# A first batch with distances and scores first, and a last output tile in two halves

## The chip, the cores and the metric

The kernel runs on one NeuronCore of a Trainium2 chip. The metric is the device time of one execution in microseconds (us), the median over several executions.

## The reference, cut to what matters

```python
# q, k, v: [8 batches, 8 heads, 576 positions, 64]; window 128
scores = q @ k.T / 8 + slopes[h] * -(i - j)        # ALiBi: a slope for each head
scores = where(0 <= i - j < 128, scores, -1e9)     # causal, sliding window
attn   = softmax(scores)
x      = (attn @ v) as [8 * 576, 8 * 64]           # 4608 tokens x 512
h      = x @ w_in                                  # 512 -> 2048
out    = (h * cos(h)) @ w_out                      # 2048 -> 512, float32
```

## The kernel before

Attention and the two matrix products of the feed-forward part are one stream of work. A batch's attention is nine *units*: four pairs of heads times two halves of the sequence (G = 0 and 1, 256 positions each), and one unit `"t"` for the last 64 positions of all heads. A unit is scores (TensorE, line 486, or 477 for the tail), exponential (ScalarE, line 516 or 508), multiplication by a table that holds ALiBi and the window (VectorE, line 532 or 525), P·V (TensorE, lines 564 and 567), division by the row sum (VectorE, lines 602 and 604), and a turn into the transposed tokens `xT` (TensorE, line 632, and a copy; later by DMA). The feed-forward part goes by nine chunks of 512 tokens: `moe1` (line 668; `moe1_half`, line 691, for chunk 0, in halves of 256 tokens) gives h, ScalarE takes its cosine, VectorE multiplies, and `moe2` (line 714) makes four output tiles of 128 tokens x 512 columns, each copied from PSUM (lines 720, 722) and stored (line 726).

For batches 0 and 1, q and k come as rows (`load_qk`, line 321) and are transposed on TensorE against an identity matrix `ident` (`qk_transposes`, line 434; copies in lines 448 and 449). Batch 0 comes in two pieces for each of q and k: positions 0 to 255 and 256 to 575. The first piece is all that the four units of G = 0 need; the others need both.

The table `EM` of ALiBi and window comes from a matrix of distances `dif` (GpSimd, lines 375 to 382), by eight exponentials on ScalarE (line 404) and copies on VectorE (lines 409 and 414). All loads are issued by GpSimd, in the order in which the program records them. They convert float32 to bfloat16 on the way.

The order on the other engines isn't the program's: `Plan.schedule` is a list scheduler that runs when the program is built. Each operation has a cost (`occ`, the time it holds its engine, and `lat`, the time to its result), a priority `pri` (lower first) and dependencies by names of buffers; the scheduler keeps a model of when each engine is free and when transfers land (`WIRE0`, `lat` of the loads), and repeatedly takes what can start first. Where an operation may run on ScalarE or VectorE, it also picks the engine. `emit` then writes the engines' programs in that order, with semaphores. So a changed cost changes no work, but may change an order. PSUM's eight banks are named `SB` (scores, four), `UB` (P·V, two) and `OB` (output tiles, two).

Of the kernel before, what the change touches and what calls it, by code (L numbers as in the profile page):

```python
# [7 lines left out]
ACTF = mybir.ActivationFunctionType  # L8
# [3 lines left out]
B, H, S, D = 8, 8, 576, 64  # L12
# [22 lines left out]
class Plan:  # L35
# [2 lines left out]

    SWITCH = 95
    TABLE = 1330  # L40
    WIRE0 = 3700

    def __init__(self, nc, ctx):
        self.nc, self.ctx = nc, ctx
# [41 lines left out]


    def schedule(self):
        free = {e: 0 for e in ENG}
        wire = {e: self.WIRE0 for e in ENG}  # L90
        mode, table = 0, None
        tables = sorted({o.table for o in self.all if o.table is not None})
        left = {t: sum(o.table == t for o in self.all) for t in tables}
        avail = []

        def reach(o, e):
            t = 0
            for d, data in o.preds.items():
                if data == ORDER or self.held(d, data, e):
                    t = max(t, d.start + d.occ)  # L100
                elif d.dma is None and d.eng[0] == e:
                    t = max(t, d.end + 28)
                else:
                    t = max(t, d.end + (53 if e == "pe" else 36))
            return t
        for o in self.all:
            if o.npred == 0:
                avail.append(o)
        order = []
        while avail:  # L110
            phase = next((t for t in tables if left[t]), None)
            best = None
            for e in ENG:
                cand = []
                for o in avail:
# [12 lines left out]
                key = (st, o.pri, o.seq)  # L128
                if best is None or key < best[0]:
                    best = (key, e, o)  # L130
            (st, _, _), e, o = best
            avail.remove(o)
            if o.table is not None and o.table != table:
                st += self.TABLE
            if len(o.eng) > 1:
                o.fn, o.occ, o.lat = o.fn[e], o.occ[e], o.lat[e]
                o.eng = (e,)
            o.start = st
            free[e] = st + o.occ
# [101 lines left out]
def bass_alibi_sliding__then__act_gcu_kernel(  # L241
# [8 lines left out]
    with ExitStack() as ctx:  # L250
# [62 lines left out]
        def piece_keys(which, b, n):  # L313
            return [("qB", which, 0), ("qB", which, 1)] if b else [("qB", which, n)]

        def load_qk(which, src, b, n=0):
            t0, R, _ = PIECES[b][n]
            c0 = 64 * (t0 // 32)
            rows = bass.AP(src.tensor, src[b].offset + 64 * t0,
                           [[64 * R, 32], [64 * S, H], [1, 64 * R]])  # L320
            op("pool", [lambda e: e.dma_start(qB[which][:, :, c0:c0 + 64 * R], rows)],  # L321
               w=piece_keys(which, b, n), dma=f"ld{which}{n}", occ=800, lat=161 * R)

        def load_v(b, order=range(NBLK)):
            for t in order:
                rows = 128 if t < 4 else 64
                op("pool", [lambda e, t=t, rows=rows: e.dma_start(  # L327
                    vp[b % 2][0:rows, t, :, 0:64],
                    v[b, :, 128 * t:128 * t + rows, :].rearrange("h p d -> p h d"))],
                   r=[("vinit", b % 2)], w=[("v", b % 2, t)], dma=f"ldv{b % 2}{t}",  # L330
                   occ=900, lat=7 * rows)

        def load_nat(which, src, b):
            fns = []
# [31 lines left out]
               w=[("wo", u)], dma=f"wo{u}", occ=800, lat=2650)  # L366


        def constants():
            sel = ["sel"]  # L370
            op("pool", lambda e: e.memset(ident[:, :], 1.0), w=["ident"] + sel)
            op("pool", lambda e: e.affine_select(
                ident[:, :], ident[:, :], pattern=[[1, 128]], compare_op=ALU.is_equal,
                fill=0.0, base=0, channel_multiplier=-1), r=["ident"], w=["ident"] + sel, occ=350)
            op("pool", lambda e: e.iota(dif[:, :, :], pattern=[[128, 2], [-1, 128]], base=-128,
                                        channel_multiplier=1,
                                        allow_small_or_imprecise_dtypes=True),
               w=["dif"] + sel, occ=350)
            op("pool", lambda e: e.affine_select(
                dif[:, 0, :], dif[:, 0, :], pattern=[[-1, 128]], compare_op=ALU.is_ge,  # L380
                fill=-1.0e6, base=-1, channel_multiplier=1), r=["dif"], w=["dif"] + sel, occ=350)
            op("pool", lambda e: e.affine_select(
                dif[:, 1, :], dif[:, 1, :], pattern=[[1, 128]], compare_op=ALU.is_ge,
                fill=-1.0e6, base=0, channel_multiplier=-1), r=["dif"], w=["dif"] + sel, occ=350)
# [35 lines left out]
        def qk_transposes(b, which, n, part, banks):  # L420
# [8 lines left out]
            def f(e):  # L429
# [6 lines left out]
                                qB[which][:, y, c0 + 64 * j:c0 + 64 * j + 64], ident[:, :])  # L436
                return ins
            num = jj[1][1] - jj[0][0]
            op("pe", f, r=piece_keys(which, b, n) + ["ident"], w=[("B", x) for x in banks],
               occ=56 * num if b else 110 * num, lat=56 * num + 170 if b else 110 * num + 250,  # L440
               mode=2, pri=3)
            for i, (j0, j1) in enumerate(jj):
                o = tr[which][b % 2][:, :].rearrange("p (k t) -> p k t", k=NPAIR)[
# [237 lines left out]
        def moe1_half(c, hf, f2, bank):  # L681
# [6 lines left out]
            for i in range(2):  # L688
# [15 lines left out]
               r=[("cos", ci)], w=[("B", bank)] + [("g", gi, 2 * f2 + i, hf) for i in range(2)],  # L704
               occ=606, lat=692, pri=3)

        def moe2(c):
            gi = c % 2
            for t in range(4):
                tg = 4 * c + t  # L710
                bank = OB[tg % 2]
                oi = tg % NOB
                for fc in range(NFC):
                    op("pe", lambda e, t=t, fc=fc, bank=bank: e.matmul(  # L714
                        ps[:, bank, :], gT[gi][:, fc, 128 * t:128 * t + 128], w_out[:, fc, :],
                        start=(fc == 0), stop=(fc == NFC - 1)),
                       r=[("g", gi, fc, t // 2), ("wo", fc // 4)], w=[("B", bank)], occ=216, lat=379,
                       pri=6)
# [13 lines left out]
        def attention(us, phase):  # L732

            for g in range(0, len(us), 2):
# [6 lines left out]
                else:  # L741
# [2 lines left out]
                        exps(u, n, 2 * phase + 2)  # L744
                    for u in two:
                        mask(u)
                sets = [list(zip(two, UB))]
                if any(u[1] == "t" for u in two):
                    sets = [[s] for s in sets[0]]
                for set_ in sets:  # L750
# [13 lines left out]


        load_qk("q", q, 0, 0)
        load_qk("k", k, 0, 0)
        constants()
        load_qk("q", q, 0, 1)
        load_qk("k", k, 0, 1)  # L770
        load_v(0)
        masks()
        for n in range(2):
            qk_transposes(0, "q", n, 0, OB)
            qk_transposes(0, "k", n, 0, OB if n else UB)
        for u in range(4):
            load_w_in(u)
        load_qk("q", q, 1)
# [34 lines left out]
                    load_nat("k", k, next_t)  # L813
            moe2(c)
        R.schedule()
        R.emit(final=[f"st{i}" for i in range(NOB)])

# [1 line left out]
_INS = ['q', 'k', 'v', 'moe_w_in', 'moe_w_out']  # L819
# [24 lines left out]
```

The softmax here doesn't subtract the row's maximum and nothing guards it: scores larger than these inputs give would overflow.

## Time and profile before

| | |
|---|---|
| time, median of 3 | 321.82 us (321.12 to 321.84) |
| span of the profiled execution | 319.1 us |
| TensorE busy | 306.3 us, 96% of the span |
| ScalarE busy | 204.1 us, 64% |
| VectorE busy | 187.5 us, 59% |
| GpSimd busy | 95.8 us, 30% |
| moved by DMA | 37.82 MB, 119 GB/s over the span |

The profile shows one execution. Engines are PE (TensorE), PEld (its weight loads), DVE (VectorE), ACT (ScalarE), POOL (GpSimd) and SP. A row of 40 digits gives the busy share of an engine in tenths, a digit for each fortieth of the span (8 us here). In a line of the timeline stand the start in us, the duration in us, engine, line of the kernel, operation, and what is written from what; "[1.69 <-DMA ...]" is the time that the engine sat idle before it, and what ended that wait. "x16" is a count. [...] matmuls in a row overlap: 128x512 ones last 379 ns and follow each other every 216 ns.

### The profile page before, as it was taken

The numbers are of one execution on the slowest core, as the hardware profiler recorded it, in microseconds if no ns is written. First come the engines' busy times: TensorE is split into PE (matmuls) and PEld (weight loads), VectorE is DVE, ScalarE is ACT, GpSimd is POOL, SyncE is SP. The second block draws the span as 40 slices with busy tenths as digits, with TensorE's granted clock in tenths as the row PEclk, the third lists the DMA queues.
The fourth block names the chain that finished last, engine by engine and source line by source line (L and its number), as shares of the span: only waits on it lengthen the run. The fifth ranks groups of instructions, "written<-read, shape, count | busy, mean of one in ns | idle before, by whom it ended". The sixth has DMA issues, their size and how long they took to land.

```text
span 319.1 us, 6207 instructions
## 1 busy us (share of the span) xinstructions
PE 306.3 (96%) x2450; PEld 152.9 (48%) x2450; DVE 187.5 (59%) x413; ACT 204.1 (64%) x297; POOL 95.8 (30%) x123
## 2 busy tenths in 40 slices
PE   2799999999999999999999999999999999999995
PEld 2468745445544554455445444544444444444442
DVE  3788758776686777669775656655653650334000
ACT  5697866886688696966678567665674662443211
POOL 7997142254537581564508100000000000000000
PEclk9999999999999999999999999999999999999999
DMA  6999999999999999999999992131022001101121
GB/s 89 179 207 210 204 160 192 146 153 169 177 123 163 167 190 150 178 164 180 125 140 148 136 147 68 55 69 44 2 73 68 34 0 68 66 0 68 66 93 71
DMA packets 144476, 37.82 MB, mean 119 GB/s; under 512 B 134208, under 2 KB 139328, under 8 KB 144448
## 3 DMA queue, kind: packets, MB, share of 16 engines
q0 software_dynamic: 99616, 18.36, 78.1%
q1 hardware_dynamic: 44832, 19.08, 29.0%
q8 instruction: 19, 0.31, 0.4%
q14 instruction: 9, 0.07, 0.1%
HBM read 36.70 MB, written 9.44 MB: 145 GB/s over the span
## 4 chain that ended last, share of the span: by engine, by line
PE 90%; DMA 6%; POOL 1%; issue 1%; DVE 0%; ACT 0%; POOLq 0%; ACTq 0%
PE ps L714 40%; PE ps L668 35%; DMA qrows<-in_q_dram 6%; PE ps L486 5%; PE ps L564 3%; PE ps L691 2%; PE ps L567 2%; PE ps L434 1%; PE ps L632 1%; PE ps L477 1%; PE ps L551 1%; PE ps L553 1%; POOL w_inb L357 1%; POOL qrows L321 0%; POOL krows L321 0%
## 5 line engine op out<-in xcount | busy, mean ns | idle before, releaser
L714 PE MATMUL ps<-w_outb,gT 128*128 128x512 bf16 x576 | 138.8, 379 | 0.0
L668 PE MATMUL ps<-xT,w_inb 128*128 128x512 bf16 x512 | 116.8, 379 | 0.4 <-DVE xnat L604 0.3
L677 DVE TENSOR_TENSOR gT<-ps,cos 128x512 bf16<-128x512 f32 x128 | 81.0, 685 | 50.2 <-PE ps L714 41.1
L673 ACT ACTIVATE cos<-ps,halfpi 128x512 f32<-128x512 f32 x128 | 81.3, 687 | 37.8 <-PE ps L714 18.6
L714 PEld LDWEIGHTS ps<-w_outb,gT 128*128 128x128 bf16 x576 | 53.7, 98 | 58.7 <-issue 1.9
L668 PEld LDWEIGHTS ps<-xT,w_inb 128*128 128x128 bf16 x512 | 47.2, 98 | 61.2 <-DVE gT L677 6.0
L516 ACT ACTIVATE p<-ps 128x768 bf16<-128x768 f32 (+1 forms) x64 | 55.6, 919 | 22.3 <-PE ps L486 18.6
L532 DVE TENSOR_TENSOR p<-p,emask 128x768 bf16<-128x768 bf16 (+1 forms) x64 | 38.3, 615 | 7.3 <-ACT p L516 6.9
L327 POOL DMA_DIRECT2D vp<-in_v_dram x40 | 33.8, 872 | 23.0 <-PE ps L567 12.2
L720 ACT ACTIVATE ob<-ps 128x512 f32<-128x512 f32 x25 | 15.0, 599 | 37.1 <-PE ps L714 37.0
L337 POOL DMA_DIRECT2D qnat<-in_q_dram x30 | 25.2, 875 | 28.8 <-DMA qt<-qnat 28.8
L337 POOL DMA_DIRECT2D knat<-in_k_dram x30 | 25.3, 877 | 27.6 <-DMA kt<-knat 25.2
L604 DVE TENSOR_TENSOR xnat<-ps,rec 128x256 bf16<-128x256 f32 x64 | 24.4, 420 | 0.7 <-DVE rec L602 0.4
L486 PE MATMUL ps<-qt,kt 64*128 64x128 bf16 (+1 forms) x320 | 19.0, 243 | 0.7 <-ACT p L516 0.7
L602 DVE RECIPROCAL rec<-ps 128x4 f32<-128x4 f32 x64 | 8.2, 168 | 18.1 <-PE ps L567 17.8
L564 PEld LDWEIGHTS ps<-vp,p 128*128 128x128 bf16 x256 | 15.4, 97 | 7.0 <-issue 3.5
L564 PE MATMUL ps<-vp,p 128*128 128x65 bf16 x256 | 18.2, 193 | 0.2 <-DVE p L532 0.2
L486 PEld LDWEIGHTS ps<-qt,kt 64*128 64x128 bf16 x320 | 11.2, 95 | 12.4 <-issue 5.1
L567 PE MATMUL ps<-vp,p 128*128 128x65 bf16 x192 | 17.0, 193 | 0.0
L691 PE MATMUL ps<-xT,w_inb 128*128 128x256 bf16 x128 | 16.0, 273 | 0.3 <-ACT xT L641 0.3
L722 DVE COPY ob<-ps 128x512 f32<-128x512 f32 x11 | 7.6, 689 | 12.7 <-PE ps L714 12.7
L567 PEld LDWEIGHTS ps<-vp,p 128*128 128x128 bf16 x192 | 13.3, 97 | 0.6
(51 smaller groups left out, 166.7 us busy)
## 6 DMA issues: line engine op xcount, KB each, us to landing
out_dram<-ob SPq DMA_DIRECT2D x36, 256.0 KB, 2.1
vp<-in_v_dram POOLq DMA_DIRECT2D x32, 128.0 KB, 9.1
qnat<-in_q_dram POOLq DMA_DIRECT2D x24, 128.0 KB, 7.2
knat<-in_k_dram POOLq DMA_DIRECT2D x24, 128.0 KB, 5.0
w_inb<-in_moe_w_in_dram POOLq DMA_DIRECT2D x4, 512.0 KB, 10.3
w_outb<-in_moe_w_out_dram POOLq DMA_DIRECT2D x4, 512.0 KB, 22.1
qrows<-in_q_dram POOLq DMA_DIRECT2D x1, 576.0 KB, 15.1
krows<-in_k_dram POOLq DMA_DIRECT2D x1, 576.0 KB, 17.1
```

What stands on the lines that cost most here:

```text
L327: op("pool", [lambda e, t=t, rows=rows: e.dma_start(vp[b % 2][0:rows, t, :, 0:64], v[b, :, 128 * t:128 * t + rows, :].rearrange("h p d -> ...
L337: fns.append(lambda e, t=t, rows=rows: e.dma_start(nat[which][0:rows, t, :, :], src[b, :, 128 * t:128 * t + rows, :].rearrange("h p d -> p ...
L486: ins = e.matmul(ps[:, banks[x], c0:c1], keys_ap(b, x, pr, kc), query_ap(b, x, pr, qb, 128 * nb), start=True, stop=True)
L516: op("act", lambda e: e.activation(P[i][:, :, lo:512], src_[:, :, lo:512], ACTF.Exp, scale=0.125), w=held + [("P", i)], occ=920 if G else ...
L532: op("dve", lambda e: e.tensor_tensor(P[i][:, :, lo:512], P[i][:, :, lo:512], EM[:, h0:h1 + 1, lo:512], ALU.mult), r=[("P", i), ("EM", h0) ...
L564: ins = e.matmul(o, P[i][:, x, d0:d0 + 128], V[:, kc, h, 0:65], start=True, stop=not two)
L567: ins = e.matmul(o, P[i][:, x, p0:p0 + 128], V[:, kc - 1, h, 0:65], start=False, stop=True)
L604: op("dve", lambda e: e.tensor_tensor(o, U[:, :, :, 0:64], rv[:, :, :, None].broadcast_to([128, 2, 2, 64]), ALU.mult), r=[("rec", n % 2)], ...
L668: op("pe", lambda e, kc=kc: e.matmul(ps[:, bank, :], w_in[:, kc, 128 * fc:128 * fc + 128], xT[:, kc, r0:r0 + CH], start=(kc == 0), stop=(k ...
L673: op("act", lambda e: e.activation(cosb[ci][:, :], ps[:, bank, :], ACTF.Sin, bias=halfpi[:, 0:1]), r=["halfpi"], w=[("B", bank), ("cos", c ...
L677: op("dve", lambda e: e.tensor_tensor(gT[gi][:, fc, :], ps[:, bank, :], cosb[ci][:, :], ALU.mult), r=[("cos", ci)], w=[("B", bank), ("g", ...
L714: op("pe", lambda e, t=t, fc=fc, bank=bank: e.matmul(ps[:, bank, :], gT[gi][:, fc, 128 * t:128 * t + 128], w_out[:, fc, :], start=(fc == 0 ...
```

## The change

It has three parts. First, GpSimd makes the distances right behind the first two loads and the identity only behind the third load, and the transposes of the second pieces of batch 0 are made to wait for the copies of the first k piece, so that scores of the first units come ahead of them; the first P·V pair uses banks `OB` instead of `UB`, and the k transposes always use `UB`. The aim is to begin attention on the first pieces while the second are on their way. Second, the scheduler's model of the start is changed: the times at which engines begin (`BEGIN`), TensorE operations that take twice as long in the first 18.5 us (`COLD`), and some costs. These are numbers for the scheduler and no work on the chip. Third, the last output tile is computed in two halves of 256 columns in two banks, each with a copy and a store of its own (`moe2_last`), so that the first half is copied and stored while the second is computed.

```diff
-    WIRE0 = 3700
+    WIRE0 = 3450
+    BEGIN = {"pe": 1000, "act": 2100, "dve": 1000, "pool": 1330, "sp": 1000}
+    COLD = 18500
...
-        free = {e: 0 for e in ENG}
+        free = dict(self.BEGIN)
...
+            if e == "pe" and st < self.COLD:
+                o.lat += o.occ
+                o.occ *= 2
...
-        def constants():
-            sel = ["sel"]
-            op("pool", lambda e: e.memset(ident[:, :], 1.0), w=["ident"] + sel)
+        def identity():
+            op("pool", lambda e: e.memset(ident[:, :], 1.0), w=["ident"], occ=290)
...
+        def distances():
             op("pool", lambda e: e.iota(dif[:, :, :], pattern=[[128, 2], [-1, 128]], base=-128,
...
-            op("pe", f, r=piece_keys(which, b, n) + ["ident"], w=[("B", x) for x in banks],
-               occ=56 * num if b else 110 * num, lat=56 * num + 170 if b else 110 * num + 250,
+            op("pe", f, r=piece_keys(which, b, n) + ["ident"] + (
+                   [("tr", "k", 0, j) for j in (0, 4)] if n else []), w=[("B", x) for x in banks],
+               occ=58 * num, lat=58 * num + 170,
...
+        def moe2_last(c, t, oi):
+            gi, row = c % 2, CH * c + 128 * t
+            for hf, bank in enumerate((OB[1], UB[0])):
+                cols = slice(256 * hf, 256 * hf + 256)
+                for fc in range(NFC):
+                    op("pe", lambda e, fc=fc, bank=bank, cols=cols: e.matmul(
+                        ps[:, bank, 0:256], gT[gi][:, fc, 128 * t:128 * t + 128],
+                        w_out[:, fc, cols], start=(fc == 0), stop=(fc == NFC - 1)),
...
+                op("sp", [lambda e, cols=cols: e.dma_start(out[row:row + 128, cols],
+                                                           ob[oi][:, cols])],
+                   r=[("ob", oi, hf)], dma=f"sl{hf}", occ=60, lat=300)
...
-                sets = [list(zip(two, UB))]
+                sets = [list(zip(two, OB if phase < 0 and g == 0 else UB))]
...
         load_qk("q", q, 0, 0)
         load_qk("k", k, 0, 0)
+        distances()
+        load_qk("q", q, 0, 1)
+        identity()
+        load_qk("k", k, 0, 1)
         constants()
-        load_qk("q", q, 0, 1)
-        load_qk("k", k, 0, 1)
...
-            qk_transposes(0, "k", n, 0, OB if n else UB)
+            qk_transposes(0, "k", n, 0, UB)
```

More of the change, by code (lines that the diff above doesn't have):

```diff
@@ L88, in schedule @@
     def schedule(self):
-        free = {e: 0 for e in ENG}
+        free = dict(self.BEGIN)
         wire = {e: self.WIRE0 for e in ENG}
-        mode, table = 0, None
+        mode, table = 0, 0
         tables = sorted({o.table for o in self.all if o.table is not None})
@@ L321, in load_qk @@
             op("pool", [lambda e: e.dma_start(qB[which][:, :, c0:c0 + 64 * R], rows)],
-               w=piece_keys(which, b, n), dma=f"ld{which}{n}", occ=800, lat=161 * R)
+               w=piece_keys(which, b, n), dma=f"ld{which}{n}", occ=740, lat=159 * R)
         def load_v(b, order=range(NBLK)):
@@ L330, in load_v @@
                    r=[("vinit", b % 2)], w=[("v", b % 2, t)], dma=f"ldv{b % 2}{t}",
-                   occ=900, lat=7 * rows)
+                   occ=900, lat=740 * rows // 100)
         def load_nat(which, src, b):
@@ L366, in load_w_out @@
                w=[("wo", u)], dma=f"wo{u}", occ=800, lat=2650)
-        def constants():
-            sel = ["sel"]
-            op("pool", lambda e: e.memset(ident[:, :], 1.0), w=["ident"] + sel)
+        def identity():
+            op("pool", lambda e: e.memset(ident[:, :], 1.0), w=["ident"], occ=290)
             op("pool", lambda e: e.affine_select(
                 ident[:, :], ident[:, :], pattern=[[1, 128]], compare_op=ALU.is_equal,
-                fill=0.0, base=0, channel_multiplier=-1), r=["ident"], w=["ident"] + sel, occ=350)
+                fill=0.0, base=0, channel_multiplier=-1), r=["ident"], w=["ident"], occ=360)
+        def distances():
             op("pool", lambda e: e.iota(dif[:, :, :], pattern=[[128, 2], [-1, 128]], base=-128,
@@ L377, in constants @@
                                         allow_small_or_imprecise_dtypes=True),
-               w=["dif"] + sel, occ=350)
+               w=["dif"], occ=450)
             op("pool", lambda e: e.affine_select(
                 dif[:, 0, :], dif[:, 0, :], pattern=[[-1, 128]], compare_op=ALU.is_ge,
-                fill=-1.0e6, base=-1, channel_multiplier=1), r=["dif"], w=["dif"] + sel, occ=350)
+                fill=-1.0e6, base=-1, channel_multiplier=1), r=["dif"], w=["dif"], occ=430)
             op("pool", lambda e: e.affine_select(
                 dif[:, 1, :], dif[:, 1, :], pattern=[[1, 128]], compare_op=ALU.is_ge,
-                fill=-1.0e6, base=0, channel_multiplier=-1), r=["dif"], w=["dif"] + sel, occ=350)
+                fill=-1.0e6, base=0, channel_multiplier=-1), r=["dif"], w=["dif"], occ=400)
+        def constants():
             for i in range(2):
@@ L705, in moe1_half @@
                occ=606, lat=692, pri=3)
+        def moe2_last(c, t, oi):
[6 more added lines that the diff above has]
+                        w_out[:, fc, cols], start=(fc == 0), stop=(fc == NFC - 1)),
+                       r=[("g", gi, fc, t // 2), ("wo", fc // 4)], w=[("B", bank)], occ=108,
+                       lat=271, pri=6)
+                op(("act", "dve"),
+                   {"act": lambda e, bank=bank, cols=cols: e.activation(
+                       ob[oi][:, cols], ps[:, bank, 0:256], ACTF.Copy),
+                    "dve": lambda e, bank=bank, cols=cols: e.tensor_copy(
+                        ob[oi][:, cols], ps[:, bank, 0:256])},
+                   w=[("B", bank), ("ob", oi, hf), ("ob", oi)],
+                   occ={"act": 281, "dve": 320}, lat={"act": 384, "dve": 405}, pri=6)
+                op("sp", [lambda e, cols=cols: e.dma_start(out[row:row + 128, cols],
+                                                           ob[oi][:, cols])],
+                   r=[("ob", oi, hf)], dma=f"sl{hf}", occ=60, lat=300)
         def moe2(c):
@@ L712, in moe2 @@
                 oi = tg % NOB
+                if tg == NTOK // 128 - 1:
+                    moe2_last(c, t, oi)
+                    continue
                 for fc in range(NFC):
@@ L815, in bass_alibi_sliding__then__act_gcu_kernel @@
         R.schedule()
-        R.emit(final=[f"st{i}" for i in range(NOB)])
+        R.emit(final=[f"st{i}" for i in range(NOB)] + ["sl0", "sl1"])
 _INS = ['q', 'k', 'v', 'moe_w_in', 'moe_w_out']
```

## The prediction

> **What bounds the kernel now.** I read the page first: how full TensorE is, and what the chain of waits is made of.
>
> ```profile
> PE   2799999999999999999999999999999999999995
> PEclk9999999999999999999999999999999999999999
> PE 90%; DMA 6%; POOL 1%; issue 1%; DVE 0%; ACT 0%; POOLq 0%; ACTq 0%
> ```
>
> TensorE is full in all slices but the first two and the last. An edit can gain only in the ramp, in the tail, or by taking work off TensorE, and none is taken off here. Next, the busy time of the first 24 us, stage by stage (columns: window, its length, then busy us and count for PE, PEld, DVE, ACT, POOL; then clock, DMA share, GB/s).
>
> ```profile
> 0.00:8.00 8.00, 2.13 (x32) 1.65 (x32) 3.04 (x14) 4.50 (x11) 6.28 (x15) 1.00 0.67 89
> 8.00:12.00 4.00, 2.41 (x36) 1.83 (x38) 2.20 (x5) 1.69 (x4) 4.00 (x6) 1.00 1.68 180
> 12.00:16.00 4.00, 3.19 (x54) 2.03 (x49) 3.68 (x11) 3.91 (x7) 4.00 (x7) 1.00 1.90 179
> 16.00:20.00 4.00, 3.25 (x58) 2.02 (x59) 3.85 (x10) 3.81 (x7) 4.00 (x6) 1.00 1.24 207
> 20.00:24.00 4.00, 4.00 (x63) 3.49 (x60) 3.26 (x12) 3.69 (x5) 4.00 (x6) 1.00 1.24 207
> ```
>
> In the first 20 us TensorE is busy 2.13 + 2.41 + 3.19 + 3.25 = 10.98 us and idle 9.0 us; then it is full. The timeline of the start says what it waits for.
>
> ```profile
> 2.87 0.22 POOL L371 MEMSET ident<- 128x128 bf16 x1
> 3.16 0.29 POOL L372 TENSOR_SCALAR_AFFINE_SELECT ident<-ident 128x128 bf16<-128x128 bf16 x1
> 3.52 0.35 POOL L375 IOTA dif<- 128x256 f32 x1
> 4.45 0.29 POOL L382 TENSOR_SCALAR_AFFINE_SELECT dif<-dif 128x128 f32<-128x128 f32 x1
> 4.90 0.75 POOL L321 DMA_DIRECT2D qrows<-in_q_dram  x1 [0.15 <-issue]
> 5.26 1.07 PE L434 MATMUL ps<-ident,qrows 128*64 128x128 bf16 x16 [5.26 <-DMA qrows<-in_q_dram]
> 8.48 0.68 DVE L449 COPY kt<-ps 128x512 bf16<-128x512 bf16 x1
> 9.29 1.28 PE L434 MATMUL ps<-ident,qrows 128*64 128x128 bf16 x20 [1.69 <-DMA qrows<-in_q_dram]
> 10.50 0.82 PE L486 MATMUL ps<-qt,kt 64*128 64x256 bf16 x8
> ```
>
> GpSimd works off five constants between its second and third load, so the third load is issued at 4.90. The first scores could run at 9.16 (8.48 + 0.68), but the transposes of the second q piece stand ahead of them and wait for that load until 9.29; the scores start at 10.50. Two narrower looks: the DMA rate just before the third load's data, and TensorE's waits on DMA after 20 us.
>
> ```profile
> 6.75:7.00 0.25, 0.25 (x10) 0.25 (x8) 0.24 (x1) 0.25 (x2) 0.25 (x1) 1.00 0.00 0
> 7.00:7.25 0.25, 0.25 (x10) 0.25 (x8) 0.25 (x1) 0.25 (x3) 0.25 (x2) 1.00 0.43 51
> ```
> ```profile
> 28.62 0.58 PE L434 MATMUL ps<-ident,qrows 128*64 128x128 bf16 x14 [0.17 <-DMA qrows<-in_q_dram]
> ```
>
> The DMA engines stand still before 7.0: the load issued at 4.90 moves its first bytes at about 7.1. And at 28.62 TensorE, full until then, waits again for a load, batch 1's q rows (issued 13.52, landing 15.1 us later). So early on there are two clocks, TensorE's own chain and the stream of loads, and they meet at 28.6. The tail in the timeline:
>
> ```profile
> 304.71 11.17 PE L714 MATMUL ps<-w_outb,gT 128*128 128x512 bf16 x51
> 315.98 0.60 ACT L720 ACTIVATE ob<-ps 128x512 f32<-128x512 f32 x1 [2.86 <-PE ps L714]
> ```
>
> After the last matmul (315.88) come a 0.60 us copy, to 316.58, and the store; the span ends at 319.13. In slices of 0.1 us the store's bytes flow from 317.4 to 318.25, so of its 2.5 us some 0.8 is movement and 1.7 is not.
>
> [...] 4.90 to 7.1 before bytes move on the load, 1.7 us on the store; halving a store can save only its bytes. [...] transposes of 314 ns mean until 12.8 us, 216 ns at best later; eight score matmuls take 0.82 us at 10.5 and 0.56 at 12.84.
>
> **The change part by part.**
>
> *GpSimd's order.* Distances now stand right behind the first two loads and ident behind the third. Ahead of the third load are dropped the rows from 2.87 to 3.52, 0.65 us; it is issued at 4.90 − 0.65 = 4.25, say 4.3. The last select of dif ends at 4.74 − 0.6 = 4.15. Ident: third issue until 5.05, 0.22 and 0.29 with gaps, ready at 5.65; the fourth load goes at 5.8 instead of 5.65.
>
> *First transposes.* They wait for ident, 5.65 instead of 5.26: +0.4. The k ones, bound by landing at 6.54 before, follow at 6.6: +0.1. Hidden: the copies behind them on ScalarE wait for the eight mask exponentials (2.56 us), which now start at 4.2 instead of 4.78.
>
> *Scores ahead of the second pieces.* Exponentials end at 6.75; VectorE's q copy (0.67) runs 7.1 to 7.8, half a tail mask (0.28), k copy (0.68) to about 8.75. Scores at 8.8 instead of 10.50: −1.7. It is not all kept. The exponentials of units 0 and 1 (1.55 together) run 9.3 to 10.85, and behind them in ScalarE's order the second q copy (0.88), units 2 and 3 (1.5), the second k copy to about 14.0, where before it was 13.76. The four kt/qt copies that the 128x1024 units need thus come no earlier. But the first P·V, now in banks 0 and 1 and not waiting for the second k copies, goes at 12.5 (before 13.59), and the masks of units 2 and 3 end at 13.0 and about 15.3, so the second P·V goes at 15.3 (before 16.51) and the third at 18.9 (before 19.75). TensorE is 0.85 to 1.2 us ahead there. Four w_in matmuls are done by then instead of six, 2 x 0.109 = 0.22 back. It reaches the full stretch 0.65 to 1.0 us earlier.
>
> *The load stream.* With the third load 0.6 us earlier the stream restarts 0.6 earlier (6.5 instead of 7.1). All later loads queue behind it: latencies of 5.3 us (v), 6.6 to 13.0 (w_in), 15.1 (q rows of batch 1) show that bytes, not issue, set them, so the 0.15 us later issue of the fourth is hidden. All land 0.6 earlier, q rows at 28.0. TensorE, at least 0.65 ahead, waits there for them. So the ramp gives the smaller clock, 0.6. The order places 64 w_in matmuls (0.109 each) ahead of that wait instead of 65, so one is left for later: −0.6 + 0.1 = −0.5 us.
>
> *The middle.* The same instructions in nearly the same order: the runs of like matmuls come to 354 before and 356 after, of which one is the new shape at the end. TensorE is full there; taken as 0.
>
> *The tail.* 16 matmuls of 512 columns, 15 x 0.216 + 0.379 = 3.62 us, become 32 of 256: 31 x 0.109 + 0.273 = 3.65, +0.03 (20 such in a row took 2.29 us in the chain). The first half's copy and store lie beside the second half's matmuls. The last copy has 256 columns: the 512 take 0.599, and the slope on ScalarE between 768 and 1024 columns is about 0.22 us per 256, so 0.38: −0.22. The nearest row, the 128x256 bf16 copy of 0.39, agrees. The store's movement of 0.8 us halves if it goes by bytes: −0.4; if it goes by the number of rows, 128 either way, 0. I take it by bytes, since the rate of the store reaches 0.45 MB per us while it lasts. Sum −0.59, between −0.2 and −0.6.
>
> Together −0.5 − 0.59 = −1.09, and 321.82 − 1.09 = 320.7.
>
> **The rivals.**
> (a) Forecast: stream and tail, 320.7. Chance 0.52.
> (b) The ramp's gain is lost again: TensorE loses it to waits for VectorE and ScalarE in the reordered middle[...]. For: the new ramp leaves TensorE idle 12.8 to 14.05 and 16.5 to 17.2, where the old one was nearly full from 9.3 to 14; and DVE is busy 5.68 of 6 us from 24 to 30. Against: the wait at 28.62 absorbs a few tenths. The tail alone stays, −0.3 to −0.7: about 321.3, the same within 0.3%. Chance 0.29.
> (c) More: the 1.2 us lead at the second P·V comes through. For: TensorE is that far ahead by its own chain. Against: the loads would have to land 1.2 us earlier too, and GpSimd issues only 0.6 earlier. −1.2 − 0.6 = −1.8: 320.0. Chance 0.12.
> (d) Slower: [...] Chance 0.07.
>
> **How the numbers follow.** The bound for faster is 0.3% of 321.82, 0.97 us, so 320.85: (a) lies just beyond it, so that a small loss in the middle or a store that saves less leaves it short; I give 0.44 of its 0.52 to faster, since the three times before (321.12, 321.82, 321.84) have their median next to the highest. With (c)'s 0.12 that is 0.56 faster, then 0.37 same (0.29 and 0.08), 0.07 slower. The range of 319.7 to 321.8 takes in (c) with the tail at its best, and (b) with the tail at its least; (d) and the edges of the others are left out.
>
> **What would show it.** Right: third load issued at 4.3 and scores at 8.8; q rows of batch 1 landing at 28.0 with a longer TensorE wait before their transposes than 0.17; last copy of 0.38 and 0.3 us less between its end and the span's end. Wrong: transposes of 314 ns beyond 13 us (d, b); q rows still at 28.6 (the stream wasn't bound by the issue at 4.90); TensorE idle in the middle (b); a store that takes as long for half its bytes.

## The result, and the profile after

| | before | changed |
|---|---|---|
| median of 6 | 321.65 us (321.12 to 321.91) | 323.12 us (322.76 to 325.36) |
| span of the profiled execution | 319.1 us | 321.0 us |

The ratio of changed to before is 1.006, with a 95% interval of 1.0031 to 1.0089, where I forecast 1.1 us less. It is the ratio of the means, 323.54 and 321.61 us, and one execution of 325.36 weighs in it; the medians are 1.5 us apart, a ratio of 1.0046. So the loss is 1.5 us by medians and 1.9 by means, and the experiments below are read both ways where that matters. Lines of the changed kernel stand further down: 321 is 326, 434 is 442, 486 is 495, 691 is 700, 714 is 748. From the page of the changed kernel:

```profile
PE   2699999998999999999999999999999999999996
PEclk9999999999999999999999999999999999999999
PE 82%; DMA 9%; POOL 4%; SPq 2%; DVE 1%; issue 1%; ACT 1%; POOLq 0%; ACTq 0%
```

TensorE's row has an 8 in the tenth place, at 72 to 80 us, where before there were only 9s; and the chain has more DMA (9% instead of 6%) and SyncE's queue (2%) in it. Three stages of the start, columns as in the prediction:

```profile
8.00:12.00 4.00, 2.78 (x36) 1.87 (x36) 2.61 (x7) 2.83 (x5) 4.00 (x6) 1.00 1.41 143
12.00:16.00 4.00, 2.76 (x40) 2.13 (x40) 2.78 (x7) 2.47 (x5) 4.00 (x7) 1.00 2.02 173
16.00:20.00 4.00, 3.93 (x42) 2.32 (x41) 3.62 (x12) 2.72 (x4) 4.00 (x6) 1.00 1.24 206
```

Read counts beside busy times here. From 12 to 20 us TensorE is busy 2.76 + 3.93 = 6.69 us for 82 matmuls; before it was 6.44 us for 112. The busy time looks the same and is 30 matmuls poorer: the matmuls themselves take longer. And from 8 to 12 us the loads move 143 GB/s where they moved 180. The timeline of the start:

```profile
4.37 0.73 POOL L326 DMA_DIRECT2D qrows<-in_q_dram  x1 [0.15 <-issue]
5.10 0.34 POOL L375 MEMSET ident<- 128x128 bf16 x1
5.51 0.29 POOL L376 TENSOR_SCALAR_AFFINE_SELECT ident<-ident 128x128 bf16<-128x128 bf16 x1
5.75 0.74 POOL L326 DMA_DIRECT2D krows<-in_k_dram  x1
5.95 1.07 PE L442 MATMUL ps<-ident,qrows 128*64 128x128 bf16 x16 [5.95 <-POOL ident L376]
9.11 0.82 PE L495 MATMUL ps<-qt,kt 64*128 64x256 bf16 x8 [1.25 <-DVE kt L458]
12.24 1.28 PE L442 MATMUL ps<-ident,krows 128*64 128x128 bf16 x20 [0.35 <-DMA krows<-in_k_dram]
14.32 0.32 PE L573 MATMUL ps<-vp,p 128*128 128x65 bf16 x3 [0.80 <-issue]
29.90 0.75 PE L442 MATMUL ps<-ident,qrows 128*64 128x128 bf16 x20 [0.50 <-DMA qrows<-in_q_dram]
```

GpSimd does what was wanted: the third load goes out at 4.37 instead of 4.90, and the scores start at 9.11 instead of 10.50. But the second k piece keeps TensorE waiting at 12.24. The first P·V starts at 14.32, later than before (13.59). The profile calls that wait "issue", yet the last of the two v blocks that it needs lands on its last engine at 14.23. And batch 1's q transposes, at 28.62 before, are at 29.90, again with TensorE waiting for the rows. So the loads are late. Two slices of 1 us from the windows of the changed kernel:

```profile
8.00:9.00 1.00, 0.00 (x0) 0.00 (x0) 1.00 (x4) 0.50 (x1) 1.00 (x2) 1.00 0.87 117
9.00:10.00 1.00, 0.89 (x12) 0.58 (x14) 0.25 (x1) 0.35 (x1) 1.00 (x3) 1.00 0.98 150
```

Before, these two slices moved 190 and 211 GB/s. Here the loads move less (and the DMA share, the last but one figure, is 0.87 and 0.98 where it was 1.17 and 1.20) although the second k piece and the first v blocks have been issued. The trace holds a landing for each of the 16 DMA engines. The second k piece lands between 10.53 and 10.84 before, and between 10.21 and 12.20 after: the quickest engine is 0.3 us earlier, the slowest 1.4 us later. The lateness stays in the loads behind it: w_in's first quarter lands at 16.59 to 18.63 (before 16.91 to 17.21), batch 1's q rows at 27.00 to 29.86 (before 27.31 to 28.57), and for TensorE's wait the last landing counts: it starts on them at 28.62 before, 0.05 us after it, and at 29.90 here, 0.04 after it. (The trace does not name the engine of a landing, so that it is the same engine that stays late is likely and not shown.)

TensorE's own chain is late as well, and not by waiting. Here is the stretch from its first matmul to batch 1's q transposes, before and after; it holds the same matmuls but for one of w_in:

```profile
5.26:28.62 23.36, 19.44 (x282) 14.66 (x283) 19.27 (x50) 19.18 (x33) 23.36 (x30) 1.00 1.37 190
5.95:29.90 23.95, 20.71 (x280) 15.59 (x280) 19.89 (x51) 17.96 (x26) 23.95 (x30) 1.00 1.36 187
```

TensorE is idle for 3.2 us instead of 3.9, and busy for 1.3 us longer. Its matmuls are slow for longer: before, transposes take 314 ns up to 12.6 us, and from 13.07 on all durations are short. After, a 128x256 matmul of line 700 still takes 0.42 us at 18.82, and short ones (0.28) begin at 19.51. Without the wait for the q rows TensorE would have been at their transposes at 29.40 instead of 28.45, 0.95 us later; the rows themselves come 1.29 us later. In this execution the rows come last, by 0.5 us.

The second place where time is lost is at 73 us. From SyncE's timeline, before, and then after:

```profile
50.57 5.60 SPq L346 DMA_TRANSPOSE qt<-qnat  x1
56.22 1.29 SPq L349 DMA_TRANSPOSE qt<-qnat  x1
57.56 5.73 SPq L346 DMA_TRANSPOSE kt<-knat  x1
```
```profile
51.68 5.79 SPq L351 DMA_TRANSPOSE qt<-qnat  x1
57.50 1.27 SPq L354 DMA_TRANSPOSE qt<-qnat  x1
58.82 0.59 SPq L760 DMA_DIRECT2D out_dram<-ob  x1
59.46 7.16 SPq L351 DMA_TRANSPOSE kt<-knat  x1
```

The schedule of the changed kernel has an output store between batch 2's q and k turns, where before it came behind both. The k turn starts 1.9 us later than before and lasts 1.4 us longer. The last of kt lands at 73.45 instead of 71.05, and TensorE waits for it, as its waits after 20 us say (the first of two lines; the second is the wait at 29.90):

```profile
PE ps L495 <- DMA kt<-knat: 0.9, 1, 0.9
PE ps L442 <- DMA qrows<-in_q_dram: 0.5, 1, 0.5
```

The chains of the two profiled runs give the account by position. Batch 1's transposes come 29.90 − 28.62 = 1.28 us later; the first w_out matmul 39.93 − 38.54 = 1.39; the 14 w_out matmuls behind the wait at 73 us 74.00 − 71.60 = 2.40, and this stays through the middle (101.95 − 99.55 = 2.40). The end comes 321.0 − 319.1 = 1.9 later, so the tail gives about 0.5 back. From the timeline of the tail:

```profile
314.66 3.66 PE L722 MATMUL ps<-w_outb,gT 128*128 128x256 bf16 x32
316.67 0.38 ACT L728 ACTIVATE ob<-ps 128x256 f32<-128x256 f32 x1 [1.15 <-PE ps L722]
317.08 2.08 SPq L734 DMA_DIRECT2D out_dram<-ob  x2
318.41 0.38 ACT L728 ACTIVATE ob<-ps 128x256 f32<-128x256 f32 x1 [1.36 <-PE ps L722]
```

The last copy is 0.38 us instead of 0.60, ending at 318.79, and the span ends 2.2 us later instead of 2.5.

### The profile page after: what moved, and what is told of

The parts are those of the page before. It is cut to its first block, busy times and chain, and to the rows that moved or that the text cites. A ratio compares the mean times of both kernels' runs of the same rounds, so it can differ in the third digit from the quotient of the medians.

```text
span 321.0 us, 6239 instructions
## 1 busy us (share of the span) xinstructions
PE 307.9 (96%) x2466; PEld 155.4 (48%) x2466; DVE 190.2 (59%) x418; ACT 203.6 (63%) x293; POOL 96.0 (30%) x123
## 4 chain that ended last, share of the span: by engine, by line
PE 82%; DMA 9%; POOL 4%; SPq 2%; DVE 1%; issue 1%; ACT 1%; POOLq 0%; ACTq 0%
PE ps L748 37%; PE ps L677 31%; DMA qrows<-in_q_dram 5%; PE ps L495 4%; PE ps L700 2%; SPq L351 2%; PE ps L573 2%; DMA kt<-knat 2%; DMA xT<-xnat 2%; PE ps L576 1%; POOL vp L332 1%; PE ps L641 1%; PE ps L722 1%; POOL w_inb L362 1%; PE ps L442 1%; PE ps L486 1%
## 5 line engine op out<-in xcount | busy, mean ns | idle before, releaser
L748 PE MATMUL ps<-w_outb,gT 128*128 128x512 bf16 x560 | 135.5, 379 | 0.0
L748 PEld LDWEIGHTS ps<-w_outb,gT 128*128 128x128 bf16 x560 | 52.1, 98 | 56.6 <-issue 1.9
L525 ACT ACTIVATE p<-ps 128x768 bf16<-128x768 f32 (+1 forms) x64 | 55.7, 917 | 26.8 <-PE ps L495 22.2
L754 ACT ACTIVATE ob<-ps 128x512 f32<-128x512 f32 x23 | 13.8, 601 | 34.0 <-PE ps L748 33.9
L495 PE MATMUL ps<-qt,kt 64*128 64x128 bf16 (+1 forms) x320 | 19.7, 251 | 2.2 <-DVE kt L458 1.2
L573 PEld LDWEIGHTS ps<-vp,p 128*128 128x128 bf16 x256 | 15.9, 99 | 8.0 <-issue 3.7
L573 PE MATMUL ps<-vp,p 128*128 128x65 bf16 x256 | 18.7, 196 | 0.9 <-issue 0.8
L576 PE MATMUL ps<-vp,p 128*128 128x65 bf16 x192 | 17.5, 195 | 0.0
L756 DVE COPY ob<-ps 128x512 f32<-128x512 f32 x12 | 8.3, 688 | 13.1 <-PE ps L748 13.1
L576 PEld LDWEIGHTS ps<-vp,p 128*128 128x128 bf16 x192 | 13.7, 98 | 0.5
```

Of the source, the lines that this page charges most:

```text
L495: ins = e.matmul(ps[:, banks[x], c0:c1], keys_ap(b, x, pr, kc), query_ap(b, x, pr, qb, 128 * nb), start=True, stop=True)
L525: op("act", lambda e: e.activation(P[i][:, :, lo:512], src_[:, :, lo:512], ACTF.Exp, scale=0.125), w=held + [("P", i)], occ=920 if G else ...
L573: ins = e.matmul(o, P[i][:, x, d0:d0 + 128], V[:, kc, h, 0:65], start=True, stop=not two)
L576: ins = e.matmul(o, P[i][:, x, p0:p0 + 128], V[:, kc - 1, h, 0:65], start=False, stop=True)
L748: op("pe", lambda e, t=t, fc=fc, bank=bank: e.matmul(ps[:, bank, :], gT[gi][:, fc, 128 * t:128 * t + 128], w_out[:, fc, :], start=(fc == 0 ...
```

## The experiments

All ratios are to the kernel before, run beside each on the same chip; its own medians in the three sets were 321.26, 321.49 and 321.65 us. Where an edit concerns an order, the finished orders of all other engines were left exactly as they were. A profile shows one execution, and some show waits of 0.7 to 2.1 us later on, at 116 to 119 or 155 to 157 us, that others of nearly the same orders don't; so the profiles are read for the places that an edit concerns, and the medians for the time.

**The tail alone.** The kernel before with `moe2_last` and no other edit.

```diff
+                if tg == NTOK // 128 - 1:
+                    moe2_last(c, t, oi)
+                    continue
```

> The kernel before with the two-halves tail alone; every other engine's order is that of before. Theory L (the loads, split by the identity, land late and cost the ramp 1.3 us; a reordered store costs 1.0 us at 73 us; the tail gains) expects 0.5 to 0.6 us less than before, because from the last matmul to the end of the span the changed kernel took 0.55 us less. Rival C (the TensorE clock stays at half rate longer) says the same of the tail: it tells the two apart only by fixing how much the rest must lose (about 2.0 us).

Measured: 320.74 against 321.26 us, ratio 0.9984 (0.9976 to 0.9992), so 0.52 us less. The tail does what it was meant to, and the rest of the change must lose about 2.0 us.

**The load order alone.** The kernel before, GpSimd's seven operations put in the changed order. (In its permutation: 0 and 1 are identity, 2 to 4 the distances, 5 and 6 the second q and k pieces.)

```diff
         R.schedule()
+        first = [o for o in R.order if o.eng[0] == "pool"][2:9]
+        at = R.order.index(first[0])
+        R.order = [o for o in R.order if o not in first]
+        R.order[at:at] = [first[i] for i in (2, 3, 4, 5, 0, 1, 6)]
         R.emit(final=[f"st{i}" for i in range(NOB)])
```

(The key `sel`, which tied the seven to one another in the program, is taken out for this.)

> The kernel before with GpSimd's seven operations alone put in the changed order (distances, second q piece, identity, second k piece); all other engines keep the order of before. Theory L: the second k piece and the v blocks land late and unevenly, batch 1's q rows at 29.5 to 30 instead of 28.6, and the time is 1.0 to 1.5 us above before. Rival C (clock): the loads are no cause, batch 1's q rows land at 28.0 to 28.6, and the time is within 0.4 us of before.

Measured: 322.75 against 321.26 us, ratio 1.0042 (1.0014 to 1.0071), 1.5 us more. The second k piece lands at 10.11 to 12.42. From TensorE's timeline and its waits in this run (its lines are one lower than in the kernel before):

```profile
8.91 1.28 PE L433 MATMUL ps<-ident,qrows 128*64 128x128 bf16 x20 [1.06 <-DMA qrows<-in_q_dram]
30.29 0.75 PE L433 MATMUL ps<-ident,qrows 128*64 128x128 bf16 x20
PE ps L485 <- DMA kt<-knat: 0.9, 1, 0.9
```

The first line is batch 0's second q piece. Batch 1's q rows land last at 30.25, 1.7 us later than before, and TensorE starts on them at 30.29 with no wait in front (0.03 us idle): here its own chain and the rows are level, both late. Its slow matmuls go on until 20 us. The wait for kt is here too, without the moved store: in the kernel before, late loads alone can bring it. So one reordering of seven GpSimd operations is enough for a loss as large as the whole result.

**The changed kernel with the old load order.** The same edit the other way, with `(4, 5, 0, 1, 2, 3, 6)` on the changed kernel.

> The changed kernel with GpSimd's seven operations put back in the order of before (identity, distances, then the second q and k pieces back to back); all else is the changed kernel's order. Theory L: batch 1's q rows land at about 28.6 again and the time falls by 1.0 to 1.4 us from the changed kernel (ratio to before about 1.001). Rival C: transposes last 314 ns until 18 us as in the changed kernel, TensorE reaches batch 1's transposes at 29 or later whatever the loads do, and the time falls by less than 0.5 us.

Measured: 321.70 against 321.26 us, ratio 1.0015 (1.0 to 1.003); from the changed kernel's 1.006 that is some 1.4 us less, by the medians (0.44 us above before instead of 1.47) 1.0. The second k piece lands at 10.43 to 10.98. Slow matmuls end at 14.5 us instead of 19. It is still 1.0 us above the tail alone (321.70 − 320.74), so a second loss is left in the order of the other engines: with the loads in time TensorE still waits 1.3 us for kt, at 72.8 us.

**The clock.** The changed kernel with work for TensorE in the time when it waits for its first data.

```diff
+        def warmup(e):
+            for _ in range(10):
+                ins = e.matmul(ps[:, SB[3], :], warm[:, 0:128], warm[:, :], start=True, stop=True)
+            return ins
+        op("pe", warmup, r=["warm"], w=[("B", SB[3])], occ=2150, pri=0)
```

> The changed kernel with ten 128x512 matmuls on a constant tile put ahead of the first transposes, where TensorE waits anyway (they write a bank that nothing reads). Theory L: transposes become short (216 to 280 ns) from the start or from 9 us, but the late loads still set batch 1's transposes at 29.5 to 30, and the time moves by less than 0.4 us. Rival C: with the clock up from the start the ramp is repaired and the time falls by 1.0 us or more.

Measured: 324.47 us, ratio 1.008 (1.005 to 1.011). That is no gain on the changed kernel's 1.006, and rather a loss, though the intervals overlap. Its windows (PEclk is the third figure from the end) show what became of the clock:

```profile
7.00:9.00 2.00, 0.19 (x8) 0.03 (x2) 2.00 (x5) 0.83 (x2) 2.00 (x3) 0.99 1.05 143
9.00:10.00 1.00, 0.91 (x12) 0.60 (x14) 0.22 (x1) 0.36 (x1) 1.00 (x3) 0.50 0.92 124
20.00:22.00 2.00, 2.00 (x34) 1.41 (x33) 1.18 (x3) 1.59 (x2) 2.00 (x3) 0.50 1.24 206
```

With the extra matmuls ahead of them the first transposes last 220 ns mean instead of 314. Then TensorE waits 1.9 us for the k copies, and from 9 us PEclk is 0.50 until after 22 us, some three us beyond the place where matmuls get short in the changed kernel (about 19). (The profiled execution also has a wait of 2.1 us for kt at 118.6 us, so that not all of its 325.04 us belongs to the start.) So the run doesn't give the clock's share in the changed kernel: its first transposes are short, and from 9 to 22 us PEclk is 0.50. Theory L's number (a move of less than 0.4 us) and rival C's (1.0 us less) are both missed by it.

**The store moved, too.** The changed kernel with the old load order, and the store back behind the k turn (the kernel before has it one place further back, behind the turn of the tail).

```diff
+        sp = [o for o in R.order if o.eng[0] == "sp"]
+        turn = next(o for o in sp if o.dma == "trk0")
+        store = sp[sp.index(turn) - 1]
+        R.order.remove(store)
+        R.order.insert(R.order.index(turn) + 1, store)
```

> The changed kernel with the old load order (as the earlier run) and with one output store moved back behind batch 2's k turns on SyncE's queue, where the kernel before has it. Theory S (the store between the two turns delays kt, for which TensorE waits at 73 us) expects about 0.5 to 1.0 us less than the old load order alone, so 320.7 to 321.2, level with the kernel before with the new tail (320.74). Rival: the wait for kt comes from the late loads alone, and moving the store gives less than 0.3 us.

Measured: 321.03 against 321.49 us, ratio 0.999 (0.9977 to 1.0002). That is 0.46 us below before, where the tail alone was 0.52 below. With both orders undone, what remains of the change besides its tail (scores first, banks, the other orders) is worth nothing that can be seen. In the start, though, the order with scores first does what it was to do once the loads are in time: the first two P·V are at 13.12 and 15.38 (before 13.59 and 16.51), and TensorE is ready for batch 1's q rows at 27.74 (28.54 − 0.80), 0.7 us earlier than before. There it waits for them:

```profile
28.54 0.64 PE L442 MATMUL ps<-ident,qrows 128*64 128x128 bf16 x16 [0.80 <-DMA qrows<-in_q_dram]
```

**The store alone moved.** The same edit on the changed kernel, loads as changed.

> The changed kernel with nothing but the one output store moved back behind kt on SyncE's queue. If the store alone makes TensorE's wait for kt at 73 us: 0.7 to 1.0 us below the changed kernel, about 0.5 us above before. If late loads bring that wait as well (as in the load order alone, where TensorE waited 0.9 us for kt without this store): 0.2 to 0.5 us below the changed kernel.

Measured: 321.82 against 321.65 us, ratio 1.0017 (0.9999 to 1.0035), from 1.006. That is some 1.4 us (1.3 by the medians; the two intervals just overlap), more than either expected. In its profile TensorE waits nowhere for kt, which has landed at 71.91, and for nothing else after 20 us. Yet the loads are as late as ever (second k piece 10.21 to 12.40), and the start is no quicker:

```profile
30.19 0.75 PE L442 MATMUL ps<-ident,qrows 128*64 128x128 bf16 x20
5.95:30.19 24.24, 21.62 (x280) 16.79 (x280) 19.70 (x50) 17.80 (x25) 23.94 (x30) 1.00 1.35 186
```

Batch 1's q rows have landed at 29.17 and TensorE comes to them at 30.19 without a wait: it was busy for 21.6 us with what took 19.4 before, slow matmuls (0.42 us for 128x256) going on until 22 us. So in this execution what comes last is TensorE's own chain, and in the changed kernel's it was the rows.

Undoing the loads gave 1.4 us, undoing the store 1.4, and both together 2.2 (1.006 to 0.999); by the medians 1.0, 1.3 and 1.9. That both together give less than the sum is within the noise of these intervals, so whether the two losses overlap is open.

**Why is the second k piece late?** Four orders of GpSimd's operations on the kernel before, with the same edit as above and another permutation, and one without VectorE's copies. Two theories stand against each other in the expectations. Q: the k piece is issued too shortly before the stream of loads gets to it. P: VectorE's bf16 copies of the table make it late, a guess from the timing alone: in the changed kernel four of them run from 5.01 to 7.49 us, and the k piece is issued at 5.75. First, identity behind both second pieces: `(2, 3, 4, 5, 6, 0, 1)`.

> The kernel before with GpSimd's order: distances, then the second q and k pieces back to back, then identity. Theory Q: the second k piece is queued in time again, its landings on the 16 engines lie within 0.4 us of each other, and all loads land 0.3 to 0.6 us earlier than before (q rows of batch 1 at 28.0 to 28.4); the first transposes wait for identity until about 6.5. Time from 0.5 below to 0.2 above before. Theory P: [...] landings spread over 1 us or more, and the time is 1 us or more above before.

Measured: 320.92 against 321.49 us, ratio 0.9974 (0.996 to 0.9989), 0.57 us less. The second k piece is issued at 5.11 (before 5.65, changed order 5.75) and lands at 9.99 to 10.59. The same two slices as above:

```profile
8.00:9.00 1.00, 0.59 (x14) 0.35 (x11) 0.96 (x3) 0.74 (x2) 1.00 (x2) 1.00 1.17 193
9.00:10.00 1.00, 1.00 (x20) 0.92 (x20) 1.00 (x3) 0.11 (x1) 1.00 (x3) 1.00 1.27 186
```

No pause, the loads 0.2 to 0.5 us ahead of before, batch 1's q rows at 28.19 instead of 28.57. TensorE starts its first transposes at 6.6 instead of 5.26, and it doesn't matter.

Second, the load order alone again, with VectorE's table copies as another operation, for theory P.

```diff
-                    op("dve", lambda e, h=h: e.tensor_copy(
-                        EM[:, h - 1:h + 1, 256:512], EM[:, h - 1:h + 1, 0:256]),
+                    op("dve", lambda e, h=h: e.tensor_tensor(
+                        EM[:, h - 1:h + 1, 256:512], EM[:, h - 1:h + 1, 0:256],
+                        EM[:, h - 1:h + 1, 0:256], ALU.max),
...
```

> The kernel before with the changed load order alone (as the earlier run, 322.75), and VectorE's six bf16 table copies written as the maximum of the tile with itself, the same values. Theory P [...]: the second k piece lands on all engines within 0.5 us, batch 1's q rows at 28.6 or earlier, and the time falls to 321.0 to 321.5. Theory Q (lead alone): landings as uneven as in that run, spread of 1.5 us or more, and the time stays at 322.3 to 323.2.

Measured: 322.71 against 321.49 us, ratio 1.0058 (1.0034 to 1.0081), and the piece at 10.08 to 12.47: as uneven as with the copies. So the unevenness doesn't need them.

Third, all four q and k loads first: `(5, 6, 0, 1, 2, 3, 4)`.

> The kernel before with GpSimd's order: all four q and k loads, then identity, then distances; other engines as before. Theory Q (each load that is not queued well ahead of the stream's reaching it lets DMA engines run dry, unevenly): the second q piece follows the first k piece without the pause at 6 to 7 us, but the v blocks, issued at the same 6.4, are now reached with little lead, and land unevenly; batch 1's q rows land between 27.5 and 29.5, time within 0.8 us of before. Theory P [...] expects all loads about 1.1 us earlier, q rows at 27.5 and the time 0.5 to 1 us below before.

Measured: 321.83 against 321.49 us, ratio 1.0007 (0.9994 to 1.0021). The second q piece lands at 7.93 to 9.02, the quickest engine 1.0 us earlier than before, the slowest 0.2. The v blocks add little unevenness of their own, the w_in quarters some; batch 1's q rows are at 28.64, and the distances are late. Neither theory had that the q piece itself would be uneven although it was issued early, at 2.88.

Fourth, identity between the two second pieces again, but both early: `(5, 0, 1, 6, 2, 3, 4)`.

> The kernel before with GpSimd's order: second q piece, identity, second k piece, distances. Identity stands between the two second pieces as in the changed kernel, but the second k piece is issued at about 4.1, some four us before the stream reaches it. Theory Q (too little lead): its landings on the 16 engines add less than 0.4 us to the spread of the q piece ahead of it. Theory R (GpSimd's own work between the two issues spoils the second): they spread by 1.0 us or more beyond it. The distances are late here, so the time says little: within 1 us of before.

Measured: 321.65 against 321.65 us, ratio 0.9998 (0.9987 to 1.0009). The q piece lands at 8.00 to 9.25, the k piece at 9.77 to 10.85: the k piece adds no spread of its own, although identity stands between. So GpSimd's work between the two issues is not enough to spoil the second one.

What goes with the unevenness of the k piece is its lead, taken as the time from its issue to the first landing of the q piece ahead of it. In the five profiled executions with the uneven piece it is 2.5 to 2.7 us, and the piece adds 1.5 to 2.0 us to the spread of the landings; in the other nine it is 3.2 to 4.3 us, and the piece adds less than 0.5. But lead isn't the whole of it: in the last two runs the q piece was issued 3.4 us before the first landing of the piece ahead (2.88 to 6.28, and 2.89 to 6.33), and yet spread over 1.1 and 1.3 us. So that a short lead is the cause is not shown. What happens inside the DMA engines, and why only some landings are late, stays open.

**What is left when both losses are out.** The kernel before with the tail and the kept pair, both as above:

> The kernel before with the two-halves tail and the kept pair (distances, second q and k pieces, identity), no other change: 0.52 and 0.57 us add, so 1.0 to 1.2 us below before, 320.1 to 320.6. If the kept pair's gain is only chance, it equals the tail alone, 0.5 below.

Measured: 320.58 against 321.65 us, ratio 0.9969 (0.996 to 0.9978), 1.07 us less: 0.52 and 0.57 add up.

The changed kernel with identity behind the pair, `(0, 1, 2, 3, 6, 4, 5)`, and the store moved back:

> The changed kernel with identity behind the second q and k pieces, and the one output store moved back behind kt. If the loads and the store are all that the changed kernel lost, this is at or below the kernel before with tail and kept pair: 320.2 to 320.9. If scores first costs something of its own (a third cause), it stays above 321.2.

Measured: 320.03 against 321.65 us, ratio 0.9954 (0.9937 to 0.9972), 1.6 us less. It is the fastest kernel of this study, better than both. Its profile is of its slowest execution, 321.50 us with a granted clock of 0.995; the other five have 0.999 or 1.0 and took 319.69 to 320.42. In that one the clock fell back in the middle of the start:

```profile
13.99:17.40 3.41, 2.27 (x39) 1.36 (x36) 3.40 (x13) 2.27 (x3) 3.41 (x6) 1.00 1.26 206
17.40:20.81 3.41, 3.41 (x45) 2.07 (x46) 2.60 (x7) 2.81 (x4) 3.41 (x5) 0.50 1.24 207
```

The interval of this kernel overlaps that of the tail with the kept pair, so that scores first has a worth of its own is likely and not shown.

## Why the prediction was wrong

*GpSimd's order and the scores.* Right in kind: issue at 4.37 (4.3 foretold), identity at 5.80 (5.65), fourth issue at 5.75 (5.8), scores at 9.11 (8.8). With the loads in time TensorE was 0.7 us ahead at batch 1's q rows, as foretold (0.65 to 1.0).

*The load stream: the step that failed.* I wrote: "bytes, not issue, set them, so the 0.15 us later issue of the fourth is hidden. All land 0.6 earlier." The q piece did come earlier, its first landing by 0.6 us and its last by 0.4. The step to the fourth load failed. The latencies that I named are those of loads behind it, and were measured in an order in which the second k piece was queued right behind the q piece. Moving the q piece ahead by 0.53 and the k piece back by 0.1 takes 0.63 of its lead away, and its last landing came 1.4 us later. In place of −0.6 the runs show +1.5 us for this order alone, and −0.57 when the pair is kept together, where the q rows of batch 1 come 0.38 earlier. The sign that I foretold was thus right for an edit that was not the one made.

*Where TensorE's chain and the stream meet (the "two clocks").* Right where the loads are in time: there TensorE waits 0.80 us for the stream, scores first can't gain more than it, and with the old load order and the store moved back the changed kernel is level with the tail alone. With the late loads it fails: the chain is late too, and comes last in the run with only the store moved. The foretold P·V at 12.5 and 15.3 (14.32 and 16.67) fell with the v blocks, which I had landing 0.6 earlier, and with the slow matmuls.

*The middle, taken as 0: the second step that failed.* I took it from TensorE's order, which is nearly unchanged, and left SyncE's out. A store of 0.59 us there, before the k turn, was worth 1.3 to 1.4 us. Before, TensorE's weight loads waited 0.5 us for that turn already: it had no slack to spare.

*The clock (rivals b and d).* The sign that I named for these two, transposes of 314 ns beyond 13 us, is in the trace: matmuls are slow until about 19 us instead of 13. (In the warm-up run transposes last 220 ns mean up to 7.2 us, 314 from 9 to 14 us, while PEclk is 0.50, and 217 to 244 from 30.5 us on, where it is 1.00. In the changed kernel a 128x256 matmul lasts 418 ns at 18.82 us while PEclk is 1.00, so that its slow matmuls mean a lower clock as well is likely and not shown.) TensorE's chain is 0.95 us later at batch 1's transposes: its first matmul comes 0.7 us later, it waits 1.0 us less, and the matmuls take 1.3 us more. What the slow matmuls cost by themselves isn't isolated, because they go with the late loads: slow matmuls end at 15.7 to 22.2 us in the five profiled executions with the uneven k piece, and at 9.6 to 15.4 in the others, but for the one in which the clock fell back. (That end moves by chance as well: before and the tail alone have the same start, and there they end at 12.6 and 15.4.) In the changed kernel's profiled execution the q rows come last by 0.5 us, so there quicker matmuls alone would have left the start where it was; in the run with only the store moved they would not. So the order of the loads is shown to be the cause by undoing it, and by which of the two paths it costs its time is open.

*The tail.* −0.59 foretold, −0.52 measured; the copy of 0.38 as foretold, and the end of the span 2.2 us after the copy instead of 2.5: the store's bytes flow for 0.5 us instead of 0.8, and 1.7 us are left as before.

*The sum.* −0.5 and −0.59 were to give −1.09. It became −0.52 for the tail and about +2.0 for the rest: the side of rival (d), slower, with the load order and the store as causes that (d) didn't name, and the slow matmuls beyond 13 us in it with a share that is open.

## What to carry to other kernels

When a load is moved forward in a queue, look at the one behind it: if the time from its issue to the moment when the stream reaches it shrinks with the move, a latency that was measured while it was well queued need not hold any longer (here that time went from 3.3 to 2.6 us, and the last landing came 1.4 us later). Where a scheduler makes the orders, compare every engine's finished order, the DMA-issuing ones first, even if the busiest engine's is unchanged. And for a load that 16 engines share, ask the trace for the first and the last landing: here a spread of 2 us was still there in loads that landed 18 us later. Where an engine looks as busy as before, compare the time that it takes for the same instructions: less waiting can hide slower work (here 6.69 us for 82 matmuls, where 6.44 us held 112).

## What the runs showed of the hardware that was not expected

- The second k piece, issued 2.6 us before the first landing of the piece ahead of it, landed over 2.0 us on its 16 engines (10.21 to 12.20); issued 3.3 us before it, over 0.3 us (before) and 0.6 us (pair kept). With 3.3 us in the fastest kernel it was 0.9. The lateness was still in batch 1's q rows, some 18 us later (last landing 29.86 instead of 28.57).
- In the warm-up run PEclk was 0.99 from 7 to 9 us and 0.50 from 9; TensorE had run matmuls from 1.53 to 7.20 us, idle for 0.1 of these 5.7 us, and then paused until 9.1. PEclk was still 0.50 from 20 to 22 us, after TensorE was recorded busy 3.69 of 4 us from 16 to 20, and 1.00 from 23. In the profiled execution of the fastest kernel it went from 1.00 to 0.50 at 17.4 us; in the 3.41 us before, TensorE was busy for 2.27 and never idle for more than 0.6 us at a time. The ten extra matmuls brought nothing: ratio 1.008 against 1.006.
- The place of seven GpSimd operations and one store moves a 320 us kernel by 1%: from 323.12 to 320.03 us with the same work.
